# Convolution and Strassen-style block: POOL and SP work around the second group put in another order

## The chip, the cores and the metric

The kernel runs on one core of one Trainium2 chip. The metric is the device time of one execution in microseconds (us). Five engines work side by side, and each runs its own instructions in order: PE (matrix products, with PEld for its weight loads), DVE (vector work), ACT (activations and copies out of PSUM), POOL (general vector work, and the issue of some transfers) and SP (only the issue of transfers). A "granted clock" below 1.00 in a row of the profile means that PE was given a lower clock in that stretch.

## The reference, cut to what matters

```
# x: (8, 4224, 192), weight: (8 heads, 7 taps)
w = softmax(weight, axis=-1)                  # seven taps for each head of 24 columns
x = sum over k of w[h, k] * x_padded[s + k]   # causal convolution along the sequence
mu, var = mean(x), mean((x - mu) ** 2)        # over the 192 columns
xn = (x - mu) / sqrt(var + 1e-6) * g_ln
out = x + maximum(xn @ w_ch1, 0) @ w_ch2      # 192 -> 768 -> 192, float32
```

## The kernel before, in words

The sequence is cut into 18 groups. A group holds up to 16 rows of the sequence on each of 128 partitions. Group 0 has 6 rows and group 1 has 8, and these two are computed with plain products; groups 2 to 17 use a scheme that saves one of eight quarter products in each matrix multiplication and pays for it with sums and differences of quarters. The order of the work on every engine is written out by hand; no scheduler moves it. The semaphores are derived from which tile an instruction reads and writes.

For one group the steps are these.

- **Load**: `load_x(g)` brings x into a tile `xg`. There are two such tiles, so x of group 4 takes the place of x of group 2. The load of the fourth x (group 3) is special (`apart=True`): three transfers on SP (lines 165 and 172), the largest with 112 partitions.
- **Convolution**: `first_tap` (line 375, ACT) writes tap 0 into `y`; `second_tap` (line 383, ACT) writes tap 1 into a tile `tb`, and `third_tap`, for group 2 alone, writes tap 2 into a part of `room`. `add_in_parts` (line 408) adds one such tile to another by four accumulating transfers that POOL issues, 384 KB each. `conv` (line 416, DVE) adds the taps that are left, one instruction for each head and tap. `y` also has two tiles; groups 0 and 1 share the first, so `first_tap(3)` must wait until `y` of groups 0 and 1 has been stored.
- **Statistics**: `moments` (DVE) and `root` (POOL), a generator: it does nine small operations, stops once (`if step == 0: yield`), and does the other ten when it is asked again.
- **Store**: `store_y` writes `y` to the output, and later `add_to_out` (line 959, POOL) adds the scaled result to it with accumulating transfers. For group 1 `store_y` is eight transfers of 96 KB, since that group lies on 16 partitions per batch.
- **First product** (`up`, `up_mixed`, `up_last`, PE line 522) and its evictions by ACT (line 512 for groups 0 and 1, line 636 after). PSUM has two sets of four banks, taken in turn, so a product can't begin before ACT has emptied the set of the product before the last one. `between(g, f)` puts pieces of `first_tap(3)` behind the evictions of `up(1)`.
- **Second product** (`down`, PE line 812, for groups 0 and 1; `down_fast`, PE line 865, after).

The quarters of the weights have sums, too: `w1sums` (three) and `w2sums` (four), made once by `sums_of_quarters` on POOL (line 572). `let_in` is a DVE memset of one element on which such a sum then waits. In `up_mixed`, `close` adds one partial product to another: mostly ACT copies the PSUM banks out and POOL issues an accumulating transfer (line 600), once DVE adds (line 642). ACT then applies the relu (line 649), DVE forms a difference (`lower_sum`, line 841), and the second product starts on these.

The change touches four places. (1) The stretch under `if g == 0` and `if g == 1` in the main loop, where the work between `up(0)` and `up_mixed(2)` is ordered. (2) `up_mixed(2)`, where POOL issues `store_y(2)` and then makes `w2sums`, ahead of the transfers of `parts_cs` and `parts_tb`. (3) `between`. (4) `up_last`, where the result of group 16 is scaled and added to the output.

Of the kernel before, what the change touches and what calls it, by code (L numbers as in the profile page):

```python
# [16 lines left out]
def kernel(  # L17
# [29 lines left out]
    nc = tc.nc  # L47
# [318 lines left out]
    def first_tap(g, heads=(0, H)):  # L366
        n = groups[g][2]
        if g == 1:

            y[g] = y[0][:, groups[0][2] :]  # L370
        elif heads[0] == 0:
            y[g] = ypool.tile([P, J, D], F32, tag="y", name=f"y{g}")
        for h in range(*heads):
            cs = slice(h * GRP, h * GRP + GRP)
            nc.scalar.mul(y[g][:, 0:n, cs], xg[g][:, 0:n, cs], taps[:, h, 0:1])  # L375
# [21 lines left out]
    def third_tap(g, heads):  # L397
        if heads[0] == 0:
            third[g] = room[:, NF * J * Q + J * D :].rearrange("p (j d) -> p j d", d=D)
        tap_products(g, third[g], 2, heads)  # L400
        if heads[1] == H:
            add_in_parts(g, tb[g], third[g])

    def add_in_parts(g, dst, src):
        n = groups[g][2]
        for js in (slice(j, min(j + 4, n)) for j in range(0, n, 4)):
            ends = [v[:, js].rearrange("p j d -> p (j d)") for v in (dst, src)]
            nc.gpsimd.dma_start(out=ends[0], in_=ends[1], accum_op=ALU.add)  # L408
# [126 lines left out]

    def between(g, f):

        if g == 1 and f >= 3:
            first_tap(3, heads=[(0, 2), (2, 4), (4, H)][f - 3])
        if g == 1 and f == 5:  # L540
            second_tap(3)

# [28 lines left out]
    def sums_of_quarters(dst, a, b):  # L571
        nc.gpsimd.tensor_tensor(dst, a, b, op=ALU.subtract)  # L572
# [29 lines left out]
    def up_mixed(g, ahead, pending):  # L602
# [73 lines left out]
        p.close(p.c21, Y, two.c22[:, 0:1])  # L676
        if g == 2:
            store_y(g, nc.gpsimd)
            sums_of_quarters(w2sums[:, 2], b12, b22)
            sums_of_quarters(w2sums[:, 0], b12, b11)  # L680
            sums_of_quarters(w2sums[:, 1], b22, w2sums[:, 0])
            sums_of_quarters(w2sums[:, 3], b21, w2sums[:, 1])
        p.product(X, s4, p.b22, False)
        p.evict(X, p.c12, True)

# [48 lines left out]
    def up_last(g, ahead, pending):  # L734


        n = groups[g][2]
        w = n * T
        hidden_tile(g)
        a = ht[g]  # L740
        a11, a12, a21, a22 = quarters_of_y(g)
        s1, s2, s3, s4 = ysums[g]
        b11, b12, b21, b22 = quarters_of_w1()
        t = [w1sums[:, k] for k in range(3)]
        (c11, c12), (c21, c22) = [
            [a[:, h, e].rearrange("p f q j t -> p f q (j t)") for e in range(2)] for h in range(2)
        ]

        def seen(banks):
            return banks[:, :, 0 : FC * w].rearrange("p q (f w) -> p f q w", w=w)  # L750

        def product(to, left, right, first=True, end=True):
            rows_of_tiles(to, left, right, first, end, True)

        def close(c, banks):
            nc.vector.tensor_tensor(c, c, seen(banks), op=ALU.add)

        Y, X = take_set(), take_set()
        product(X, a11, b11, True, False)
        nc.scalar.copy(c11, seen(X))  # L760
        for step in range(2):
            next(pending, None)
        next(ahead)
        product(Y, a12, b21)
        close(c11, Y)
        size, step = groups[g - 1][2], 4

        def scaled(j):
            scale(g - 1, j, j + 1)
            if (j + 1) % step == 0:  # L770
                add_to_out(g - 1, j + 1 - step, j + 1)

        for j1 in range(0, HJ, step):
            part, factor = ots[g - 1][:, j1 : j1 + step], rstd[g - 1][:, j1 : j1 + step]
            nc.vector.tensor_tensor(
                part, part, factor.unsqueeze(2).to_broadcast([P, step, D]), op=ALU.mult
            )
            add_to_out(g - 1, j1, j1 + step)
        product(X, s2, t[0], False, False)
        nc.scalar.copy(c21, seen(X))  # L780
        product(Y, s3, t[1], True, False)
        nc.scalar.copy(c22, seen(Y))
        nc.scalar.activation(c11, c11, AF.Relu)
        product(X, s1, b12, False, False)
        close(c22, X)
        product(Y, a22, t[2], False)
        close(c21, Y)
        product(X, s4, b22, False)
        scaled(HJ), scaled(HJ + 1)
        nc.scalar.activation(c22, c22, AF.Relu)  # L790
        scaled(HJ + 2), scaled(HJ + 3)
        nc.scalar.activation(c12, seen(X), AF.Relu)
        lower_sum(g, (PAIR, *range(PAIR)))
        kept = xpool.tile([P, J + PAD, D], F32, tag="xg", name=f"kept{g}")
        kept = kept.rearrange("p j d -> p (j d)")[:, 0 : NF * (n - fast[g]) * P]
        kept = kept.rearrange("p (j e f q h t) -> p j e f q h t", e=2, f=FC, q=NQ, h=2, t=T)
        rows_left[g] = kept.rearrange("p j e f q h t -> p j (e f) (q h t)")

        def keep(h, e, j):
            nc.scalar.activation(  # L800
                kept[:, j - fast[g], e, :, :, h], a[:, h, e, :, :, j], AF.Relu
            )

        return [lambda j=j: scaled(j) for j in range(HJ + step, size)] + [
            lambda h=h, e=e, j=j: keep(h, e, j)
            for h, e in ((0, 0), (0, 1), (1, 1), (1, 0)) for j in range(fast[g], n)
        ]
# [142 lines left out]
    def add_to_out(g, j1, j2):  # L950
        if groups[g][0] is None:

            j1, j2 = (0, j2) if j2 == groups[g][2] else (0, 0)
        for ps, rows in rows_of_out(g, j1, j2) if j2 else ():
            src = ots[g][ps, j1:j2].rearrange("p j d -> p (j d)")
            step = 4 * D if groups[g][0] is not None else (j2 - j1) * D
            for d0 in range(0, (j2 - j1) * D, step):
                d1 = min(d0 + step, (j2 - j1) * D)
                nc.gpsimd.dma_start(out=rows[:, d0:d1], in_=src[:, d0:d1], accum_op=ALU.add)  # L959
# [65 lines left out]
    b11, b12, b21, b22 = quarters_of_w2()  # L1025
    for g in range(NG):
        last = g + 1 == NG
        if g + 2 < NG and g not in (1, 2):
            load_x(g + 2)
        if g < 2:  # L1030
            up(g)
            work = []
        else:
            work = (up_last if last else up_mixed)(g, ahead(g), pending)
            pending = iter(())
        if g == 0:
            early = CH * C // GRP
            join_low(*words_2)
            conv(1, 1, 5, heads=(0, early))
            join_sign(*words_2)  # L1040
            join_product(w2flat, *words_2)
            conv(1, 5, K, heads=(0, early))
            transpose(1, 0, CH)
            conv(1, heads=(early, H))
            first_tap(2)
            second_tap(2)
            let_in(w1sums[:, 1])
            sums_of_quarters(w1sums[:, 1], w12, w22)
            sums_of_quarters(w1sums[:, 0], w11, w1sums[:, 1])
            load_x(3, apart=True, gate=True)  # L1050
            transpose(1, CH, NC)
            store_y(1)
            moments(0)
            moments(1)
            down(g)
            for step in root(0):
                pass
            continue
        if g == 1:
            conv(2, 3)  # L1060
            flat = [v.rearrange("p j d -> p (j d)") for v in (y[2], tb[2])]
            nc.vector.tensor_tensor(flat[0], *flat, op=ALU.add)
            let_in(w1sums[:, 2])
            sums_of_quarters(w1sums[:, 2], w21, w1sums[:, 0])
            load_x(4, nc.gpsimd)
            transpose(2)
            fourth_sum = sums_of_y(2, nc.gpsimd)
            nc.vector.tensor_tensor(w12, w12, w11, op=ALU.subtract)
            moments(2)
            down(g)  # L1070
            fourth_sum()
            continue
        if g + 2 < NG:
            store_y(g + 1)
        results = down_fast(g, work)
        if last:
            finish_fast(g, 1, *results)
            for j in range(fast[g]):
                add(g, j, ots[g][:, j])
            store(g, 0, fast[g])  # L1080
            for j in range(fast[g], groups[g][2]):
                rows = take_bank()[:, 0:D]
                down_row(rows, lambda f: rows_left[g][:, j - fast[g], f])
                add(g, j, rows)
                store(g, j, j + 1)
        elif g % 2 == 0:
            pending = root(g)
# [30 lines left out]
```

## Time and profile before

| what | value |
|---|---|
| three runs | 960.52, 963.00, 963.14 us; median 963.0 |
| the profiled execution | 961.25 us, of which the span is 959.5 us |
| PE busy | 943.5 us, 98% of the span |
| DVE busy | 895.2 us, 93% |
| ACT busy | 720.2 us, 75% |
| POOL busy | 352.8 us, 37% |
| mean granted clock | 0.998 |

The page gives the busy time of each engine over the whole span. The list of waits names, for each line, what ended the idle time in front of its instructions. The timeline lists instructions in order of time, with equal neighbours merged: start, duration, engine, line, operation, output and input, count, and in brackets the idle time before the first of them and what ended it. A DMA row on an engine is the issue of a transfer, not the transfer; a row's landing time says when its data had arrived. A row of a stretch of time gives the busy time of each engine in it, the granted clock, the share of time in which the 16 DMA engines were busy, and the bytes moved per time. Spans on POOL are rough: a row begins when the instruction is taken up, also while the one before it is still at work.

### The profile page before, as it was taken

How to read it: one execution, taken by the hardware profiler on the slowest of the kernel's cores; microseconds unless marked ns; L12 is line 12 of the kernel's file. 1: busy time of each engine (PE TensorE's matmuls, PEld its weight loads, DVE VectorE, ACT ScalarE, POOL GpSimd, SP SyncE). 2: the span in 40 equal slices, each digit the busy share in tenths (PEclk: the TensorE clock that was granted, in tenths of full speed). 3: DMA queues.
4: the chain of work that ended last, by engine and by line, in shares of the span. 5: the costliest groups of instructions: out<-in, count | busy, mean ns of one | idle time of the engine just before them, and what ended most of it. 6: DMA issues, size and time to landing. Idle time of an engine off the chain costs nothing.

```text
span 959.5 us, 38510 instructions
## 1 busy us (share of the span) xinstructions
PE 943.5 (98%) x17106; PEld 745.2 (78%) x17106; DVE 895.2 (93%) x1479; ACT 720.2 (75%) x1283; POOL 352.8 (37%) x464
## 2 busy tenths in 40 slices
PE   9989899999999999999999999999999999999998
PEld 7989659687786978778695877769696877869687
DVE  8999789999999999999998999999999999997886
ACT  6955687969687896968778696877879697878654
POOL 2076556142544217141452416241361424332140
PEclk9999999999999999999999999999999999999999
DMA  8388787897969798897969889797978979685623
GB/s 203 120 190 198 181 243 141 232 179 163 238 134 265 137 244 156 198 221 130 276 125 258 154 197 206 134 268 144 251 150 227 186 149 228 134 175 112 111 36 78
DMA packets 38348, 171.94 MB, mean 179 GB/s; under 512 B 4517, under 2 KB 5798, under 8 KB 32039
## 3 DMA queue, kind: packets, MB, share of 16 engines
q0 software_dynamic: 31632, 109.03, 61.1%
q1 hardware_dynamic: 6544, 60.45, 17.3%
q8 instruction: 134, 2.20, 0.9%
q14 instruction: 32, 0.26, 0.1%
q10 hardware_dynamic: 6, 0.00, 0.0%
HBM read 38.92 MB, written 50.92 MB: 94 GB/s over the span
## 4 chain that ended last, share of the span: by engine, by line
PE 88%; DVE 4%; POOL 2%; DMA 2%; issue 2%; ACT 1%; DVEq 0%; POOLq 0%; ACTq 0%
PE ps L865 44%; PE ps L522 41%; DVE y L416 3%; PE ps L812 2%; POOL w2sums L572 1%; DMA room<-parts_tb 1%; PE ps L362 1%; DMA room<-parts_cs 1%; PE ps L323 1%; DVE st L447 0%; DMA room<-room 0%; POOL room L600 0%; ACT room L649 0%; PE ps L349 0%; ACT room L636 0%
## 5 line engine op out<-in xcount | busy, mean ns | idle before, releaser
L416 DVE SCALAR_TENSOR_TENSOR y<-xg,taps,y 128x384 f32<-128x384 f32 (+3 forms) x710 | 358.3, 579 | 0.6 <-issue 0.6
L865 PE MATMUL ps<-room,w2sums 128*32 128x256 f32 (+1 forms) x4464 | 244.0, 376 | 1.1 <-ACT cs L871 1.1
L636 ACT COPY room<-ps 128x512 f32<-128x512 f32 (+1 forms) x225 | 180.6, 845 | 63.4 <-PE ps L522 62.5
L522 PE MATMUL ps<-yt,w 32*128 32x256 f32 (+3 forms) x4092 | 226.1, 365 | 1.4 <-issue 0.9
L865 PEld LDWEIGHTS ps<-room,w2sums 128*32 128x32 f32 x4464 | 146.1, 110 | 93.1 <-ACT cs L871 2.0
L522 PEld LDWEIGHTS ps<-yt,w 32*128 32x128 f32 x4092 | 203.2, 185 | 19.0 <-issue 8.0
L865 PE MATMUL ps<-room,w 128*32 128x256 f32 (+1 forms) x3456 | 193.0, 375 | 4.4 <-ACT room L649 4.4
L908 DVE TENSOR_TENSOR room<-room 128x1024 f32<-128x1024 f32 x135 | 154.6, 1218 | 19.7 <-PE ps L865 14.2
L865 PEld LDWEIGHTS ps<-room,w 128*32 128x32 f32 x3456 | 112.1, 111 | 76.9 <-ACT room L649 5.3
L959 POOL DMA_DIRECT2D out_dram<-ot x70 | 59.9, 942 | 198.8 <-ACT ot L948 186.9
L522 PE MATMUL ps<-ysums,w1sums 32*128 32x256 f32 (+1 forms) x2304 | 132.2, 371 | 0.0
L522 PEld LDWEIGHTS ps<-ysums,w1sums 32*128 32x128 f32 x2304 | 121.2, 185 | 5.3 <-issue 0.2
L948 ACT ACTIVATE ot<-ot,r 128x192 f32<-128x192 f32 x246 | 104.2, 467 | 0.0
L649 ACT ACTIVATE room<-room 128x1024 f32<-128x1024 f32 x90 | 94.9, 1064 | 12.1 <-DMA room<-parts_cs 10.1
L871 ACT COPY cs<-ps 128x256 f32<-128x256 f32 (+1 forms) x192 | 70.8, 369 | 44.1 <-PE ps L865 43.6
L408 POOL DMA_DIRECT2D y<-tb x59 | 52.3, 1381 | 112.8 <-ACT room L871 97.3
L375 ACT ACTIVATE y<-xg,taps 128x384 f32<-128x384 f32 (+3 forms) x141 | 72.7, 606 | 4.8 <-DVE y L416 4.3
L522 PE MATMUL ps<-yt,w1sums 32*128 32x256 f32 (+1 forms) x1152 | 71.7, 371 | 0.0
L522 PE MATMUL ps<-ysums,w 32*128 32x256 f32 (+1 forms) x1152 | 71.2, 369 | 0.0
L447 DVE BATCH_NORM_STATS2 st<-y 128x6 f32<-128x192 f32 x264 | 70.2, 344 | 0.0
L871 ACT COPY room<-ps 128x256 f32<-128x256 f32 (+1 forms) x96 | 35.4, 371 | 40.4 <-PE ps L865 39.8
L383 ACT ACTIVATE tb<-xg,taps 128x384 f32<-128x384 f32 (+1 forms) x120 | 65.5, 625 | 0.0
(125 smaller groups left out, 977.0 us busy)
## 6 DMA issues: line engine op xcount, KB each, us to landing
xg<-in_x_dram SPq DMA_DIRECT2D x13, 2112.0 KB, 16.3
out_dram<-ot POOLq DMA_DIRECT2D x61, 384.0 KB, 9.5
room<-room POOLq DMA_DIRECT2D x45, 512.0 KB, 5.3
y<-tb POOLq DMA_DIRECT2D x58, 384.0 KB, 8.5
out_dram<-y SPq DMA_DIRECT2D x14, 1536.0 KB, 8.7
room<-parts_cs POOLq DMA_DIRECT2D x30, 512.0 KB, 6.8
room<-parts_tb POOLq DMA_DIRECT2D x15, 1024.0 KB, 7.6
xg<-in_x_dram POOLq DMA_DIRECT2D x1, 2112.0 KB, 13.0
```

The costliest lines, as they stand in the source:

```text
L375: nc.scalar.mul(y[g][:, 0:n, cs], xg[g][:, 0:n, cs], taps[:, h, 0:1])
L383: nc.scalar.mul(dst[:, 0:n, cs], xg[g][:, k : k + n, cs], taps[:, h, k : k + 1])
L416: nc.vector.scalar_tensor_tensor(out=y[g][:, 0:n, cs], in0=t[:, k : k + n, cs], scalar=taps[:, h, k : k + 1], in1=y[g][:, 0:n, cs], op0=AL ...
L447: nc.vector.bn_stats(out=sums[g][:, j, :], in_=y[g][:, j, :])
L522: nc.tensor.matmul(banks[:, q, i * w + j1 * t : i * w + j2 * t], right[rows, c, P * i : P * i + P], left[rows, j1:j2, c, :], start=start, ...
L636: nc.scalar.activation(to, of, AF.Relu) if relu else nc.scalar.copy(to, of)
L649: nc.scalar.activation(c, c, AF.Relu)
L865: nc.tensor.matmul(dst[C * q : C * q + C, 0:w], right[:, f, C * c : C * c + C], left[:, f, q], start=(first and f == PAIR), stop=(f == PAI ...
L871: nc.scalar.copy(to[:, c], dst[:, 0:w].rearrange("p (j t) -> p j t", t=t))
L908: nc.vector.tensor_tensor(dst[:, f], left[:, f], right_of[:, f], op=op)
L948: nc.scalar.mul(ots[g][:, j, :], ots[g][:, j, :], rstd[g][:, j : j + 1])
L959: nc.gpsimd.dma_start(out=rows[:, d0:d1], in_=src[:, d0:d1], accum_op=ALU.add)
```

## The change

- `third_tap(2)` no longer issues the four transfers that add the third tap to the second; POOL now does so between the two parts of `root(0)`.
- `store_y(1)` (eight transfers) stands ahead of `load_x(3)` (three) in SP's order.
- `first_tap(3)` is cut 1, 2, 2 and 3 heads behind the evictions 2, 3, 4 and 5 of `up(1)`, where it was 2, 2 and 4 behind 3, 4 and 5.
- The third sum of w1 moves on POOL from behind the y transfers of group 3 to directly behind `root(0)`, and its `let_in` memset goes.
- x of group 4 is loaded by SP at the head of pass `g == 2`, not by POOL in pass `g == 1`.
- The four sums of w2 move on POOL from `up_mixed(2)`, behind `store_y(2)`, to the end of pass `g == 1`, ahead of all transfers of `up_mixed(2)`.
- In `up_last`, DVE scales and adds one piece of four rows of group 16, not two; the rows 4 to 7 are scaled by ACT between its copies, one place earlier than the rows behind them, which move back.

```diff
         tap_products(g, third[g], 2, heads)
-        if heads[1] == H:
-            add_in_parts(g, tb[g], third[g])
...
-        if g == 1 and f >= 3:
-            first_tap(3, heads=[(0, 2), (2, 4), (4, H)][f - 3])
+        if g == 1 and f >= 2:
+            first_tap(3, heads=[(0, 1), (1, 3), (3, 5), (5, H)][f - 2])
...
             store_y(g, nc.gpsimd)
-            sums_of_quarters(w2sums[:, 2], b12, b22)
-            sums_of_quarters(w2sums[:, 0], b12, b11)
-            sums_of_quarters(w2sums[:, 1], b22, w2sums[:, 0])
-            sums_of_quarters(w2sums[:, 3], b21, w2sums[:, 1])
...
-        for j1 in range(0, HJ, step):
-            part, factor = ots[g - 1][:, j1 : j1 + step], rstd[g - 1][:, j1 : j1 + step]
-            nc.vector.tensor_tensor(
-                part, part, factor.unsqueeze(2).to_broadcast([P, step, D]), op=ALU.mult
-            )
-            add_to_out(g - 1, j1, j1 + step)
+        part, factor = ots[g - 1][:, 0:step], rstd[g - 1][:, 0:step]
+        nc.vector.tensor_tensor(
+            part, part, factor.unsqueeze(2).to_broadcast([P, step, D]), op=ALU.mult
+        )
+        add_to_out(g - 1, 0, step)
         product(X, s2, t[0], False, False)
         nc.scalar.copy(c21, seen(X))
+        scaled(step), scaled(step + 1)
...
         product(X, s4, b22, False)
-        scaled(HJ), scaled(HJ + 1)
+        scaled(step + 2), scaled(step + 3)
         nc.scalar.activation(c22, c22, AF.Relu)
-        scaled(HJ + 2), scaled(HJ + 3)
+        for j in range(HJ, HJ + step):
+            scaled(j)
...
-        if g + 2 < NG and g not in (1, 2):
+        if g + 2 < NG and g != 1:
             load_x(g + 2)
...
             sums_of_quarters(w1sums[:, 0], w11, w1sums[:, 1])
+            store_y(1)
             load_x(3, apart=True, gate=True)
             transpose(1, CH, NC)
-            store_y(1)
             moments(0)
             moments(1)
             down(g)
-            for step in root(0):
-                pass
+            steps = root(0)
+            next(steps)
+            add_in_parts(2, tb[2], third[2])
+            next(steps)
+            sums_of_quarters(w1sums[:, 2], w21, w1sums[:, 0])
             continue
...
-            let_in(w1sums[:, 2])
-            sums_of_quarters(w1sums[:, 2], w21, w1sums[:, 0])
-            load_x(4, nc.gpsimd)
             transpose(2)
...
             fourth_sum()
+            sums_of_quarters(w2sums[:, 2], b12, b22)
+            sums_of_quarters(w2sums[:, 0], b12, b11)
+            sums_of_quarters(w2sums[:, 1], b22, w2sums[:, 0])
+            sums_of_quarters(w2sums[:, 3], b21, w2sums[:, 1])
             continue
```

## The prediction

> **What bounds the kernel now.** First the page's busy times, then the waits of PE.
>
> ```profile
> PE 943.5 (98%) x17106; PEld 745.2 (78%) x17106; DVE 895.2 (93%) x1479; ACT 720.2 (75%) x1283; POOL 352.8 (37%) x464
> PE ps L865 <- ACT room L649: 4.4, 2, 2.7
> PE ps L812 <- ACT room L512: 2.4, 1, 2.4
> ```
>
> PE is busy for all but 16 us of the span. Besides start, end and single gaps of about 1 us there are two waits: 2.4 us before the second product of group 1 and 4.4 us before that of group 2. The change touches both places. Next, PE's timeline and the clock around the larger one, and what POOL and DVE did before it.
>
> ```profile
> 111.17 0.64 PE L865 MATMUL ps<-room,w 128*32 128x256 f32 x8
> 114.55 0.64 PE L865 MATMUL ps<-room,w 128*32 128x256 f32 x8 [2.75 <-ACT room L649]
> 116.83 4.92 PE L865 MATMUL ps<-room,w 128*32 128x256 f32 x56 [1.64 <-ACT room L649]
> ...
> 117.00:120.40 3.40, 3.40 (x36) 1.74 (x32) 3.40 (x6) 3.40 (x5) 0.00 (x0) 0.50 0.56 113
> ...
> 93.56 0.87 POOL L488 DMA_DIRECT2D out_dram<-y  x1
> 94.13 10.26 POOL L572 TENSOR_TENSOR w2sums<-w 128x288 f32<-128x288 f32 x2
> 104.47 2.73 POOL L572 TENSOR_TENSOR w2sums<-w,w2sums 128x288 f32<-128x288 f32 x2
> 107.14 1.77 POOL L600 DMA_DIRECT2D room<-parts_cs  x2
> ...
> 88.09 14.88 DVE L416 SCALAR_TENSOR_TENSOR y<-xg,taps,y 128x384 f32<-128x384 f32 x28
> ...
> 98.33 1.93 ACT L636 COPY parts_cs<-ps 128x1024 f32<-128x1024 f32 x2 [0.72 <-PE ps L522]
> 104.00:108.00 4.00, 4.00 (x80) 3.79 (x76) 4.00 (x4) 3.37 (x2) 3.84 (x5) 1.00 0.00 0
> ```
>
> ACT had parts_cs out of PSUM at 100.26; POOL issued its transfers only at 107.14, since the w2 sums held it from 94.43 to 107.19. From 104 to 108 the DMA engines did nothing (share 0.00). The transfers landed at 113.36 and 115.70, the relus followed, and PE waited. The two gaps then brought a granted clock of 0.50 for 3.4 us, the only such stretch: this product's 488 matmuls took 28.23 us by the chain of waits, while 504 take 27.33 later (26.46 for 488). So this place costs 4.4 + 1.8 = 6.2 us.
>
> The smaller wait:
>
> ```profile
> 60.01 1.02 ACT L512 ACTIVATE room<-ps 128x1024 f32<-128x1024 f32 x1 [1.56 <-PE ps L522]
> 65.38 1.12 ACT L375 ACTIVATE y<-xg,taps 128x384 f32<-128x384 f32 x2 [4.34 <-DVE y L416]
> 66.41 1.00 ACT L512 ACTIVATE room<-ps 128x1024 f32<-128x1024 f32 x1
> 67.31 1.11 ACT L375 ACTIVATE y<-xg,taps 128x384 f32<-128x384 f32 x2
> 68.32 1.01 ACT L512 ACTIVATE room<-ps 128x1024 f32<-128x1024 f32 x1
> ...
> 47.30 0.81 SPq L165 DMA_DIRECT2D xg<-in_x_dram  x2
> 48.44 11.80 SPq L488 DMA_DIRECT2D out_dram<-y  x8
> ```
>
> Two evictions of up(1) stand on ACT behind first_tap(3), which started at 65.38. The row names DVE, but what it waits for there, the moments, ended at 51.9. The late ones are the stores of y: the last three were issued at 57.55 to 59.45, as each reuses a semaphore of the x transfers ahead of it, and landed by about 64.9. PE's sixth matmul of down(1) needs the last eviction (69.33); unhindered, behind five of 0.33 from the end of up(1) at 65.06, it would have run at 66.7. The place costs 2.6 us.
>
> **The change part by part.**
>
> *w2 sums (PE's second wait).* They now follow the last y sum on POOL. Removed: the hold of 94.43 to 107.19. Added at the new place: four operations of 0.66 us (the first ended at 103.64, 0.66 after DVE fell idle at 102.97) to 0.99. Where that is follows from DVE's chain, so the third sum of w1 comes first.
>
> *Third tap's transfers and the third w1 sum.* POOL runs nine root operations from 53.7 at one per 0.53 us (their spacing now, beside L416): to 58.5. Then four transfers at 0.84 (3.34/4): to 62. Ten more root operations: to 67.3. Then the w1 sum, 2.65 us. Beside DVE's running L416 it either gets in at once and holds DVE, or waits for conv(2,3) to end at 69.6; both end about 72.2. The transfers' packets needed 8.2 us of all DMA engines before (57.5 on, last landing 69.42); from about 60 that gives a landing near 71, also before 72.2. So the flat add (3.36 us, now at 69.79) starts at about 72.2: 2.4 late. In exchange L592 shrinks from 5.06 us (it lay beside this same w1 sum) to L591's 0.96, 4.1 less. So moments(2) ends 86.4, not 88.17: DVE 1.7 us early. yt is ready at 78.9 (PE wants it at 83), s2 at 80.9 (wanted at 85): cost 0.
>
> *The w2 sums there.* POOL's two y sums (1.83 each) end at about 85.9; the first w2 sum runs beside the moments, the other three meet conv(3) from 86.5. Before, the last two did the same: L416 became 1.14 instead of 0.605, 0.54 each. So POOL is free at about 89.8 and DVE loses 1.6, its lead. L600's first issue slips from 87.90 to 89.8; its relu is wanted only at 102.7 and the landing takes 8, so this is hidden. parts_cs then goes out at 98.9 and 99.9, when ACT is done. It queues behind store_y(2), whose packets end at 103.8 as now, and by the 6.2 us from issue to landing of an empty queue lands near 108 and 110. Relus at 109 and 111.3; PE wants the second at 111.17 + 0.9. Stall 0 to 1, taken as 0.2. With no gap, no half clock: **-6.0 us**, bounds -6.2 and, if the stall stays at one 2.75 us gap without the clock, -3.4.
>
> *Stores ahead of x, finer first_tap.* SP issues eight stores from 47.30 at 0.46: x leaves at 51.1 instead of 47.30. Its three transfers landed 11.8 to 12.1 after the first issue; same DMAs, so 62.9 to 63.2, and ACT starts first_tap(3) at about 63.5. Then one head (0.52), eviction 3 (0.9), two heads (1.0), eviction 4 (0.9), two heads (1.0), eviction 5 (1.0): the sixth matmul runs at start + 5.4 = 68.9 against 69.38. **-0.5 us.** But eviction 3 now stands behind the wait: PE product 5 starts at start + 1.6 = 65.1 instead of 62.4, a PE gap of 2.7. If that trips the half clock, 1.7 is lost. Bounds: -2.6 (x by 61) to +1.7 (clock) or, x landing 2 later, +1.5.
>
> *x of group 4 on SP*: issued when conv(2) ends, 69.6, while the DMA share is 0.02 (69 to 76). Landed 93.56 before, ahead of the first L600; it is used at 128.9. Worth nothing by itself; SP's next work is at 122.8, so nothing is queued behind it. The y transfers (ACT's second tap ends 74.4, 75.4 before) stand beside its tail; landing 86 to 87.5, before 86.74. conv(3) has 1.6 us of cover. 0, bounds 0 to +1.5.
>
> *up_last*: DVE loses one L775 (0.95). ACT's two 0.46 scales fit in its 0.90 idle ahead of the copy at 927.62; rows 8 to 11 fit into the 1.80 idle ahead of 936.62. The additions (0.9 on POOL) end at 942.3 as before; the span ends with L963 and a store. 0, bounds -0.9 to +0.5 (the 0.92 PE gap at 933.76 has no named cause).
>
> Sum: 961.25 - 6.0 - 0.5 = 954.8, with the half clock in up(1) 956.5. The profiled execution lies 1.75 under the median 963.0 of the runs, a spread of the size of one half-clock stretch. I take 955.8.
>
> [...] In the trace the first w2 sum waited 8.5 us through sixteen L416, while the last two got in at the next L416. [...] In the trace PE gaps of 2.75 and 1.64, split by 0.64 of work, brought the half clock. [...]
>
> **Rivals.**
> 1. *POOL is shut out by DVE (slower).* If the second w2 sum waits like the first did, until conv(3) pauses at 101.4, POOL gives L600 its first issue at about 104; the third lands near 114 instead of 100.93, ACT's eviction of c22 (103.64) waits for that, and PE stands some 10 us where it stood 4.4: 961.25 + 5 = 966. For it: the 9.50 us span. Against: back-to-back sums got in at the next instruction, and two of three start at the head of conv(3). It decides if the wait exceeds some 8 us. Chance 0.16.
> 2. *A new wait takes half of the gain*: y of group 3 lands after 89, or x after 65, or parts_cs stays behind the store; PE still stands 2 to 3 us. 961.25 - 3 = 958.5 to 961. For it: DMA share 1.03 from 85 to 98. Chance 0.18.
> 3. *The stall stays as it is*, since the sums were not what parts_cs waited for (the store in front of them ran to 103.8): 961 to 963. Against: DMA share 0.00 from 104 to 108. Chance 0.08.
>
> **How the numbers follow.** The likeliest case (0.58) has 952.5 to 958 as its own range. Rivals 2 and 3 reach to 963; with rival 1 left out the range is 952.0 to 963.0. A difference under 0.3% (2.9 us: 960.1 to 965.9) can't be told from none. Faster: 0.58 + 0.14 of rival 2 = 0.72; same: 0.04 of it and 0.08 = 0.12; slower: 0.16.
>
> **What the profile after would show.** Right: no idle row in front of the second product of group 2, no 0.50 stretch there, w2sums before the first L600, its transfers of parts_cs at 98 to 100; first_tap(3) at 63 to 64; L592 at 0.96. Wrong: a w2sums row of many us, L600 after 95, idle PE rows released by room or ps around 62 to 69 above 3 us, or conv(3) starting after 89.

## The result, and the profile after

The changed kernel takes 957.81 us (median of six runs, 955.85 to 960.04); the kernel before, run beside it, 963.07 (960.26 to 965.12). The ratio is 0.9952, with a 95% interval of 0.9929 to 0.9975: about 5 us faster. The profiled execution took 957.02 us with a span of 955.3, against 961.25 and 959.5.

The busy times of the page after:

```profile
PE 942.7 (99%) x17106; PEld 749.6 (78%) x17106; DVE 891.6 (93%) x1477; ACT 720.4 (75%) x1287; POOL 343.7 (36%) x463
```

PE is busy for 0.8 us less than before, and idle for 12.6 instead of 16. The larger new rows in the list of PE's waits after (us in total, times, longest us):

```profile
PE ps L520 <- ACT room L510: 3.5, 2, 3.2
...
PE ps L860 <- issue: 1.4, 3, 0.7
```

The two waits that stood there before, 4.4 us at the second product of group 2 and 2.4 at that of group 1, are gone. In their place there is one of 3.2 inside `up(1)`, where PE had none, and three short ones in the last second product that no engine ended. PE's timeline after shows the first of them and the mended place:

```profile
50.02 13.23 PE L520 MATMUL ps<-yt,w 32*128 32x256 f32 x240
66.41 4.50 PE L520 MATMUL ps<-yt,w 32*128 32x256 f32 x48 [3.16 <-ACT room L510]
70.84 15.87 PE L807 MATMUL ps<-w,room 128*128 128x192 f32 x96
...
111.37 2.96 PE L520 MATMUL ps<-yt,w 32*128 32x256 f32 x48
114.26 4.09 PE L860 MATMUL ps<-room,w 128*32 128x256 f32 x72
118.17 7.95 PE L860 MATMUL ps<-room,w2sums 128*32 128x256 f32 x144
```

The row of a stretch in the same profile (busy time of PE, PEld, DVE, ACT and POOL, then granted clock, DMA share, GB/s):

```profile
66.40:69.80 3.40, 3.39 (x32) 2.87 (x36) 3.40 (x5) 2.88 (x5) 3.23 (x4) 0.50 0.96 183
```

The sixth product of `up(1)` waits 3.16 us for ACT, and its 48 matmuls then take 4.50 us at a clock of 0.50, where 48 of the 288 took 2.64 before (15.82/6). In front of the second product of group 2 (114.26), and in it, there is neither an idle row nor a slow stretch. The timelines of ACT and POOL after tell why, in both places:

```profile
58.20 1.02 ACT L510 ACTIVATE room<-ps 128x1024 f32<-128x1024 f32 x1 [1.56 <-PE ps L520]
64.83 0.61 ACT L375 ACTIVATE y<-xg,taps 128x384 f32<-128x384 f32 x1 [5.61 <-POOL d L476]
65.35 1.00 ACT L510 ACTIVATE room<-ps 128x1024 f32<-128x1024 f32 x1
...
86.05 1.55 POOL L570 TENSOR_TENSOR w2sums<-w 128x288 f32<-128x288 f32 x2
87.67 1.67 POOL L570 TENSOR_TENSOR w2sums<-w,w2sums 128x288 f32<-128x288 f32 x2
90.99 0.87 POOL L598 DMA_DIRECT2D room<-room  x1 [1.65 <-ACT room L634]
...
102.73 1.76 POOL L598 DMA_DIRECT2D room<-parts_cs  x2 [5.21 <-ACT parts_cs L634]
```

The fourth eviction of `up(1)` (65.35; number 3 in the diff and the prediction, which count from 0) stands behind a first_tap(3) that started only at 64.83. The row names POOL, but the wait that ended last on ACT there, at 64.56, is on a transfer of x, as the chain of work that ended last has it:

```profile
51.73 12.80 DMA xg<-in_x_dram
64.53 0.03 ACTq L375
```

The w2 sums are done at 89.34, ahead of every addition, and `parts_cs` goes out as soon as ACT has it; it lands at 109.71 and 112.25. DVE's timeline after, for steps 2 and 3 of the prediction:

```profile
72.41 3.36 DVE L1060 TENSOR_TENSOR y<-y,room 128x3072 f32<-128x3072 f32 x1 [0.19 <-issue]
...
80.27 0.96 DVE L590 TENSOR_TENSOR ysums<-ysums,yt 128x768 f32<-128x768 f32 x1
...
82.43 4.25 DVE L445 BATCH_NORM_STATS2 st<-y 128x6 f32<-128x192 f32 x16
89.01 15.04 DVE L414 SCALAR_TENSOR_TENSOR y<-xg,taps,y 128x384 f32<-128x384 f32 x28 [2.33 <-ACT room L634]
```

PE's time cut at the places that the change touches, from the starts of the products in the timelines:

| stretch of PE | before | after | difference |
|---|---|---|---|
| start to `up(1)` | 49.24 | 50.02 | +0.8 |
| `up(1)` and `down(1)` | 34.3 | 36.6 | +2.3 |
| `up_mixed(2)` | 27.6 | 27.6 | 0 |
| second product of group 2 | 33.8 | 27.3 | -6.5 |
| groups 3 to 16 | 772.2 | 770.9 | -1.3 |
| `up_last` to PE's last matmul | 37.6 | 38.2 | +0.6 |

Together, unrounded, that is -4.2, the whole difference of the spans. The change takes out 6.5 us and gives 2.3 back, 48 us earlier. The experiments ask what each part is worth by itself, and why the sum of the parts is not the whole.

### The profile page after: what moved, and what is told of

The parts are those of the page before. It is cut to its first block, busy times and chain, and to the rows that moved or that the text cites. A ratio compares the mean times of both kernels' runs of the same rounds, so it can differ in the third digit from the quotient of the medians.

```text
span 955.3 us, 38512 instructions
## 1 busy us (share of the span) xinstructions
PE 942.7 (99%) x17106; PEld 749.6 (78%) x17106; DVE 891.6 (93%) x1477; ACT 720.4 (75%) x1287; POOL 343.7 (36%) x463
## 4 chain that ended last, share of the span: by engine, by line
PE 90%; DMA 3%; DVE 2%; POOL 2%; ACT 1%; issue 1%; SPq 0%; ACTq 0%; DVEq 0%; POOLq 0%
PE ps L860 44%; PE ps L520 41%; PE ps L807 2%; DVE y L414 2%; DMA xg<-in_x_dram 1%; DMA room<-room 1%; PE ps L362 1%; ACT room L634 1%; PE ps L323 1%; POOL room L598 0%; POOL d L457 0%; SPq L486 0%; POOL r L480 0%; POOL d L475 0%; POOL d L476 0%
## 5 line engine op out<-in xcount | busy, mean ns | idle before, releaser
L634 ACT COPY room<-ps 128x512 f32<-128x512 f32 (+1 forms) x225 | 180.6, 844 | 63.9 <-PE ps L520 62.4
L860 PEld LDWEIGHTS ps<-room,w2sums 128*32 128x32 f32 x4464 | 148.7, 110 | 90.1 <-issue 1.6
L860 PE MATMUL ps<-room,w 128*32 128x256 f32 (+1 forms) x3456 | 190.5, 373 | 0.2 <-DVE room L640 0.2
L866 ACT COPY room<-ps 128x256 f32<-128x256 f32 (+1 forms) x96 | 35.7, 372 | 40.4 <-PE ps L860 39.7
```

Source lines behind the costliest of these rows:

```text
L634: nc.scalar.activation(to, of, AF.Relu) if relu else nc.scalar.copy(to, of)
L860: nc.tensor.matmul(dst[C * q : C * q + C, 0:w], right[:, f, C * c : C * c + C], left[:, f, q], start=(first and f == PAIR), stop=(f == PAI ...
L866: nc.scalar.copy(to[:, c], dst[:, 0:w].rearrange("p (j t) -> p j t", t=t))
```

## The experiments

Each comparison had runs of the kernel before beside it; their medians were 963.59 us in the first (first four kernels), 961.50 in the second (next four) and 961.98 in the third. Ratios are to these.

### The new wait in up(1): three ways to order the same work

**x ahead of the stores again, first_tap(3) cut as before.**

```diff
-            store_y(1)
             load_x(3, apart=True, gate=True)
             transpose(1, CH, NC)
+            store_y(1)
...
-        if g == 1 and f >= 2:
-            first_tap(3, heads=[(0, 1), (1, 3), (3, 5), (5, H)][f - 2])
+        if g == 1 and f >= 3:
+            first_tap(3, heads=[(0, 2), (2, 4), (4, H)][f - 3])
```

> The changed kernel with the x transfers ahead of the stores again and first_tap(3) cut 2, 2, 4 behind evictions 3, 4, 5, all else as changed. Theory (the new order of this step is what costs: the fourth eviction of up(1) stands behind a first_tap that waits for x, PE stands 3.16 us and then runs 48 matmuls at half clock in 4.50 instead of 2.64): up(1) runs without a gap, first_tap(3) starts at about 65.5, the wait moves to the sixth matmul of down(1) with about 2, and down(1) ends near 83.6 instead of 86.7: 957.8 - 3.1 = 954.7. Rival (the transfers of the third tap, now beside x, are what makes the eviction late, whatever the order on SP): PE still loses what it lost, 957 or more.

Measured: 958.4 us, ratio 0.9947 (0.9929 to 0.9965), no better than the changed kernel. The gap did move, but it brought the slow clock with it. Timelines of PE and ACT, then the row of the stretch:

```profile
66.63 17.56 PE L807 MATMUL ps<-w,room 128*128 128x192 f32 x96 [2.58 <-ACT room L510]
...
64.55 1.12 ACT L375 ACTIVATE y<-xg,taps 128x384 f32<-128x384 f32 x2 [4.78 <-DMA out_dram<-y]
```

```profile
68.00:71.40 3.40, 3.40 (x13) 3.24 (x12) 3.15 (x4) 3.40 (x7) 1.18 (x1) 0.50 0.15 30
```

`up(1)` and `down(1)` take 36.1 us, and first_tap(3) now waits for the last stores. Undoing both halves of the step brings nothing, against my theory. The time fits the rival (957 or more), but the row names the last stores, not x, as what ACT waited for. The packets of the third tap's transfers ran beside these stores from 58.8 on; whether they made the stores late isn't shown. That they make the eviction late whatever the order on SP, as the rival has it, falls with the next kernel.

**The cut of first_tap(3) alone undone, the stores still ahead of x.** The diff is the second half of the one above.

> The changed kernel with first_tap(3) cut 2, 2, 4 behind evictions 3, 4, 5 again; the stores stay ahead of x. Theory (the place of first_tap ahead of the fourth eviction costs, not the order on SP): no gap in up(1), no half clock there, first_tap(3) still at about 64.8, the sixth matmul of down(1) at 68.8 with a gap of about 1.3, down(1) ends near 83.0 instead of 86.7: 957.8 - 3.7 = 954.1. Rival (the order on SP costs, since x lands 1.5 later than forecast): 956.5 or more.

Measured: 953.46 us, ratio 0.9899 (0.9875 to 0.9922), 4.4 under the changed kernel. Timelines of ACT and PE:

```profile
62.59 1.12 ACT L375 ACTIVATE y<-xg,taps 128x384 f32<-128x384 f32 x2 [2.38 <-POOL r L480]
...
64.67 16.16 PE L807 MATMUL ps<-w,room 128*128 128x192 f32 x96 [0.24 <-ACT room L510]
```

So the new order on SP is a gain, 4.9 us between these two kernels: first_tap(3) starts 14.2 us after the start of `up(1)` (48.42) instead of 16.6 (47.98) in the kernel above. The loss is the one head of first_tap that was put ahead of the fourth eviction: PE gets 0.24 us of waiting without it, 3.16 with it.

**The whole of first_tap(3) behind the last eviction.**

```diff
-        if g == 1 and f >= 2:
-            first_tap(3, heads=[(0, 1), (1, 3), (3, 5), (5, H)][f - 2])
+        if g == 1 and f == 5:
+            first_tap(3)
```

> The changed kernel with the whole of first_tap(3) behind eviction 5 of up(1). Theory: no eviction waits for x or for a store, PE has no gap from 50.0 to the end of down(1) at 81.8 (5.0 earlier): 957.8 - 5.0 = 952.8; ACT's first and second tap take 66.9 to 75.1, the y transfers leave at about 75.2 instead of 77.9. Rival (a new wait takes what is won: conv(3), the sums of w2 and the transfers of parts_cs were in time only because PE came late): PE stands again before the second product of group 2 or waits for y sums, 955.5 to 958.

Measured: 953.02 us, ratio 0.9893 (0.9869 to 0.9916). `up(1)` and `down(1)` take 32.1 us and the second product of group 2 27.3, so no new wait appeared. first_tap(3) starts at 65.58, and ACT is through with it and second_tap(3) at 73.8 instead of 77.6. The rival's wait is there in small in other profiles: four kernels of the last groups below share this order, and in theirs PE waits 0.3 to 1.7 us in front of that product for DVE (line 640). This and the kernel above it cannot be told apart.

### What the place of the w2 sums is worth

**The w2 sums back in up_mixed(2), all else as changed.** The four calls stand behind `store_y(2)` again.

> The changed kernel with the four sums of w2 back behind store_y(2) in up_mixed(2). Theory (these sums were what held the transfers of parts_cs): they span about 12.8 us behind the store at 97, parts_cs leaves at about 110, PE stands some 4.4 at the second product of group 2 and runs a stretch at half clock: 957.8 + 6.2 = 964.0. Rival (the store in front of the sums, or the later third tap, decides when parts_cs lands): within 1 of 957.8.

Measured: 960.01 us, ratio 0.9965 (0.9950 to 0.9980), 2.2 over the changed kernel (1.3 by the ratios) instead of 6.2. The profile shows no stall at all (timelines of POOL and PE):

```profile
97.37 7.72 POOL L570 TENSOR_TENSOR w2sums<-w 128x288 f32<-128x288 f32 x2
...
106.80 1.73 POOL L598 DMA_DIRECT2D room<-parts_cs  x2
...
114.40 4.13 PE L864 MATMUL ps<-room,w 128*32 128x256 f32 x72
```

The sums held `parts_cs` until 106.80, as before (107.14). But PE, having lost time in `up(1)`, came to the second product at 114.40 instead of 111.17, and what landed at 111.36 and 114.13 was in time. In the changed kernel the two parts cover the same stall: the loss of the one makes most of the gain of the other. The median of ten runs is still 2.2 above; that may be a stall in runs other than the profiled one, which the profile doesn't show.

**The same with PE in time (the whole of first_tap(3) last).**

> The kernel with the whole of first_tap(3) behind eviction 5, and the four sums of w2 back behind store_y(2) in up_mixed(2). Theory (with the sums there the stall was hidden only while PE came 5 us late from up(1)): parts_cs leaves near 106 and lands near 110 and 113, PE wants it at 108.6 and 109.2, stands some 4 to 5 and runs a stretch at half clock: 953.0 + 6 = 959.0. Rival (the sums' place is worth no more than the 2.2 by which the same edit moved the changed kernel): 955.2.

Measured: 958.1 us, ratio 0.9964 (0.9947 to 0.9981), 5.1 over the same kernel with the sums moved (6.8 by the ratios). The size is what the theory gave, the mechanism is another (timelines of POOL, DVE and PE):

```profile
91.38 1.87 POOL L570 TENSOR_TENSOR w2sums<-w 128x288 f32<-128x288 f32 x2
...
96.88 1.77 POOL L598 DMA_DIRECT2D room<-parts_cs  x2 [1.48 <-ACT parts_cs L634]
...
88.72 17.68 DVE L414 SCALAR_TENSOR_TENSOR y<-xg,taps,y 128x384 f32<-128x384 f32 x28 [2.34 <-ACT room L634]
...
111.37 4.09 PE L864 MATMUL ps<-room,w 128*32 128x256 f32 x72 [2.90 <-DVE room L640]
```

Here the sums got in at once between conv's instructions and were done at 95.4, so `parts_cs` was not held. They held DVE: the 28 instructions of conv(3) took 17.68 us instead of 14.91 in the kernel with the sums moved, DVE's addition L640 came that much later, and PE waited 2.90 for it, without a slow clock.

**The kernel before with the w2 sums moved, and nothing else.**

> The kernel before with one part of the change alone: the four sums of w2 stand behind the last y sum of pass g == 1. Here they meet conv(3), which starts at 88.1 as before. Theory (each sum waits for one of conv's instructions, as the last two did before): POOL is free near 91.5, the first addition goes out about 3.5 later than at 87.90 but in time, parts_cs goes out at 98 to 99, PE has no wait and no half clock at the second product of group 2: 963.6 - 6.2 = 957.4, with the 2.4 before the second product of group 1 left. Rival (POOL is shut out by DVE): a w2sums row of 8 us or more at 88 to 104, the first addition after 100, PE stands longer than before, 966 or more.

Measured: 957.6 us, ratio 0.9962 (0.9942 to 0.9981), so 3.9 under its neighbour and not 6.2. The sums meet conv(3) here, and POOL is not shut out (timelines of POOL, DVE and PE):

```profile
87.87 1.86 POOL L572 TENSOR_TENSOR w2sums<-w 128x288 f32<-128x288 f32 x2
89.81 2.06 POOL L572 TENSOR_TENSOR w2sums<-w,w2sums 128x288 f32<-128x288 f32 x2
91.82 2.64 POOL L600 DMA_DIRECT2D room<-room  x3
...
88.42 16.57 DVE L416 SCALAR_TENSOR_TENSOR y<-xg,taps,y 128x384 f32<-128x384 f32 x28
...
113.12 3.28 PE L861 MATMUL ps<-room,w 128*32 128x256 f32 x56 [0.58 <-ACT room L649]
```

conv(3) takes 16.57 instead of 14.88; three of its instructions are 1.15 long instead of 0.61. PE's second product of group 2 takes 28.3 us (27.3 free of waits), 5.5 less than before, at full clock. By the profile the part is worth 5.5, by the medians 3.9.

**The kernel before with the stores ahead of x and the finer first_tap(3), and nothing else.**

> The kernel before with one part of the change alone: the stores of group 1 ahead of x and first_tap(3) cut 1, 2, 2, 3 behind evictions 2 to 5. Theory (the two waits are not additive, as PE's delay at up(1) gives POOL's sums of w2 the time they lack): up(1) and down(1) take some 2.3 longer, PE comes about 3 later to the second product of group 2, whose stall of 4.4 and half clock of 1.8 are gone or nearly: 963.6 + 2.3 - 6 = 959.9. Rival (the two places are independent and the stall stays): 963.6 + 2.3 = 965.9.

Measured: 963.96 us, ratio 1.0013 (0.9986 to 1.0040): no gain. Against its neighbour's 961.50 that is +2.5 (by the ratio +1.3, with an interval from -1.3 to +3.8), the rival's size (+2.3) and not the theory's (-3.7). Yet the stall did not stay; the timelines of PE and POOL and the row of the slow stretch show both halves:

```profile
66.48 5.41 PE L522 MATMUL ps<-yt,w 32*128 32x256 f32 x48 [3.63 <-ACT room L512]
...
98.21 8.45 POOL L572 TENSOR_TENSOR w2sums<-w 128x288 f32<-128x288 f32 x2
...
117.27 3.06 PE L865 MATMUL ps<-room,w 128*32 128x256 f32 x52 [0.96 <-ACT room L649]
```

```profile
64.90:71.70 6.80, 5.21 (x48) 3.99 (x48) 5.49 (x10) 4.46 (x7) 1.84 (x5) 0.50 0.68 131
```

`up(1)` and `down(1)` take 38.3 us, 4.0 more than before; the second product of group 2 takes 28.7, 5.2 less, although the w2 sums stand where they stood and `parts_cs` leaves even later, at 108.35. So the theory's mechanism is there, and its sum failed by a dearer `up(1)` (3.63 of gap and a slow stretch of twice the length), and in the profile also by 1.4 in the last groups (39.0 from `up_last` to PE's last matmul, 37.6 before): here a delay of PE of 4 us at `up(1)` removes most of the stall at group 2 by itself.

### The third tap and the third w1 sum

**The best kernel so far (first_tap(3) last) with this part undone.** The four transfers stand in `third_tap` again, the sum with its `let_in` behind the y transfers of group 3.

```diff
-            next(steps)
-            add_in_parts(2, tb[2], third[2])
-            next(steps)
-            sums_of_quarters(w1sums[:, 2], w21, w1sums[:, 0])
...
+            let_in(w1sums[:, 2])
+            sums_of_quarters(w1sums[:, 2], w21, w1sums[:, 0])
```

> The kernel with the whole of first_tap(3) behind eviction 5, and the third tap's four transfers and the third sum of w1 where they were before (transfers right behind the third tap, the sum behind the y transfers of group 3, with its let_in). Theory (this part costs and gains nothing, as forecast): 953, within 1; DVE's second difference lasts about 5 instead of 0.96, the moments of group 2 end within 2 of where they did, PE does not see it. Rival (moving it is worth something now that PE comes 5 earlier): y sums late for up_mixed(2), PE waits 2 to 4 for them or conv(3) runs later than the first relu allows, 955 to 957.

Measured: 956.6 us, ratio 0.9950 (0.9930 to 0.9970), 3.6 over the kernel it came from (5.5 by the ratios). The rival held. Timelines of POOL, DVE and PE:

```profile
77.34 3.93 POOL L572 TENSOR_TENSOR w1sums<-w,w1sums 128x1152 f32<-128x1152 f32 x1
...
91.85 2.63 POOL L600 DMA_DIRECT2D room<-room  x3
...
88.45 16.57 DVE L416 SCALAR_TENSOR_TENSOR y<-xg,taps,y 128x384 f32<-128x384 f32 x28
...
86.09 1.58 PE L522 MATMUL ps<-ysums,w1sums 32*128 32x256 f32 x24 [0.36 <-POOL ysums L596]
...
113.37 3.27 PE L862 MATMUL ps<-room,w 128*32 128x256 f32 x56 [1.83 <-ACT room L649]
```

With the w1 sum in its old place POOL's y sums end at 87.9 instead of 84.1, the w2 sums meet conv(3) again, the additions start at 91.85 instead of 87.25, and PE, which is in time here, waits in `up_mixed(2)` (28.8 us instead of 27.6) and for the relu of `parts_cs`.

### The last groups

**up_last as before, with first_tap(3) last**, twice, in two comparisons.

> The kernel with the whole of first_tap(3) behind eviction 5, and up_last as before (DVE scales and adds two pieces). Theory (the last product's waits for nothing that the profile names, 1.4 to 3.3 us against 0.9 before, come with the changed up_last): the part from up_last to the end of PE takes 37.6 again instead of 40.4: 953.0 - 2.5 = 950.5. Rival (they are the load of PE's program, whose phase the rest of the kernel sets): 953.0, within 0.7.

> The kernel with the whole of first_tap(3) behind eviction 5 and up_last as before, once more, beside the one with late additions: 951.2 as it was, with 37.5 for the part from up_last to the end of PE. If the theory of the program loads holds, it is some 1.5 slower than the one with late additions; if the order on DVE and ACT decides, 2 faster.

Measured: 951.19 us, ratio 0.9891 (0.9859 to 0.9923), and 952.91, ratio 0.9914 (0.9898 to 0.9930). The nine runs have a median of 952.9.

**One place for the late additions.** In `scaled`, the second, third and fourth addition are written behind the last scaled row.

```diff
-            if (j + 1) % step == 0:
-                add_to_out(g - 1, j + 1 - step, j + 1)
+            if j + 1 == size:
+                for j1 in range(step, size, step):
+                    add_to_out(g - 1, j1, j1 + step)
```

> The kernel with the whole of first_tap(3) behind eviction 5 and the changed up_last, but its second, third and fourth addition all wait until the last row of group 16 is scaled, so that three transfers stand together behind it. Theory of the program loads: only the last loads can be late, 37 instead of 40.4 for the part from up_last to the end of PE, 949.7. Rival (it is the changed order on DVE and ACT, not the transfers): 40.4 stays, 953.

Measured: 952.32 us, ratio 0.9904 (0.9886 to 0.9922). The edit did not do what it was for. Each addition waits only for its own rows, and POOL has nothing else to do there, so the three went out at 924.09, 927.83 and 933.12, as spread out as ever. It is a second run of the kernel with first_tap(3) last; the nine runs of the two have a median of 952.5. By the times the old and the new `up_last` can't be told apart.

**Without the four additions of group 16's result** (their transfers are left out, so that group's rows lack the product).

```diff
         def scaled(j):
             scale(g - 1, j, j + 1)
-            if (j + 1) % step == 0:
-                add_to_out(g - 1, j + 1 - step, j + 1)
...
-        add_to_out(g - 1, 0, step)
```

> The kernel with the whole of first_tap(3) behind eviction 5 and the changed up_last; it leaves out the four additions of group 16's scaled rows to the output in up_last (their transfers alone, not the scaling). Theory (PE's waits in the last two products are for loads of its own program, 128 matmuls each, and these loads come late because the additions' transfers, now spread over three places, are in their way): no load is late, PE has no gap there, and the part from up_last to the end of PE takes 36.3 instead of 40.4: 953.0 - 4 = 949. Rival (the transfers have nothing to do with it): 40.4 stays, 953.

Measured: 950.2 us, ratio 0.9881 (0.9863 to 0.9900); `up_last` to PE's last matmul takes 36.5 us instead of 40.4. PE's timeline in the second product of group 17, first with the additions (the kernel with the old cut of first_tap(3), which has the same `up_last`), then without:

```profile
927.24 4.44 PE L860 MATMUL ps<-room,w2sums 128*32 128x128 f32 x139
933.10 0.31 PE L860 MATMUL ps<-room,w2sums 128*32 128x128 f32 x3 [1.42 <-issue]
...
935.21 1.58 PE L860 MATMUL ps<-sums,w2sums 128*32 128x128 f32 x49
938.21 2.71 PE L860 MATMUL ps<-sums,w2sums 128*32 128x128 f32 x91 [1.42 <-issue]
```

```profile
927.39 4.11 PE L857 MATMUL ps<-room,w2sums 128*32 128x128 f32 x144
931.32 2.15 PE L857 MATMUL ps<-room,w 128*32 128x128 f32 x72
```

What these gaps are can be read from the trace. The page after, like the page before, has the row `q8 instruction: 134, 2.20, 0.9%`: 134 packets with 2.20 MB, so 16 KB each. PE has 17,106 matmuls and as many weight loads; if the packets are loads of their program, there is one for 128 matmuls with their weight loads (17,106/134 = 127.7). That they are is inferred from the name of the queue, from this count and from the borders: in every profile PE's unexplained gaps in the last two products lie where 573, 445, 317, 189 or 62 matmuls are left (one off in one profile), so 127 or 128 apart. The packets show, against these borders, where each load starts:

| kernel | loads start with so many matmuls left | gaps at (us) |
|---|---|---|
| before | 824, 600, 541, 419, 282, 148 | 573 (0.92) |
| after | 824, 663, 495, 389, 277, 145 | 445 (0.74), 317 (0.32), 189 (0.32) |
| old cut of first_tap(3) | 828, 665, 512, 345, 209, 141 | 317 (1.42), 189 (1.42) |
| without the additions | 828, 700, 568, 436, 268, 141 | none over 0.13 |

Without the additions the first loads start within 1 to 9 matmuls of the border (701, 573, 445) and two later ones 48 and 49 behind it (268 for 317, 141 for 189), none with a gap over 0.13. With them the loads come up to 120 late (325 for 445, in the kernel with late additions; 209 for 317 in the table). That the gaps are waits for these loads shows in their ends: at each of the 27 gaps over 0.2 us in the last 50 us of the fourteen profiles, PE goes on 1.2 to 1.6 us after the end of a packet. Shown is that with the additions these loads start late. How the additions delay one is not: the packets themselves took 0.9 to 1.9 us there in all kernels. By gaps over 0.2 us the old `up_last` pays at one border in three of five profiles and at two or three in the others, the new one at two or three in seven of eight; the stretch takes 37.3 to 39.0 (five, old) against 37.9 to 40.4 (eight, new), which the medians don't repeat.

## Why the prediction was right and wrong, step by step

The forecast was 955.8, from a sum of 954.8 for the profiled execution. The runs gave 957.8 and 957.0. Direction and range hold, and so does the own range of the likeliest case (952.5 to 958), at its edge; but one step had the wrong sign and another was right for a reason that is only half of the truth. Two of its own signs of being wrong were there: an idle PE row of 3.16 released by room in front of 66.41, and conv(3) starting after 89 (89.01). That the number came within about 2 us is in part luck: step 4 was 2.8 too low, and the w2 sums (0.5) and groups 3 to 16 (1.3, in no term) gave more than forecast.

1. **w2 sums, -6.0.** Measured -6.5 at that place, with everything that was named: no idle row, no 0.50 stretch, sums ahead of the first addition, `parts_cs` out when ACT is done (102.73, and not 98 to 100, since PE and ACT were 3 us later), landings in time. But the term was added as if it were independent of step 4. With the sums back the place loses 0.15 us by the profile as long as PE is late (27.48 against 27.33); alone in the kernel before the move is worth 5.5 by the profile and 3.9 by the medians. A delay of PE at `up(1)` and the relief of POOL pay for the same stall. The sum of the whole change isn't hurt by this, since with the sums moved there is no stall left for the delay to hide and it counts in full in step 4; but neither term is what its part is worth alone. By the ratios moving the sums is worth 1.3 us with PE late (0.9952 against 0.9965) and 6.8 with PE in time (0.9893 against 0.9964). The two parts alone moved the medians by -3.9 and +2.5, which makes -1.4, and the whole change by -5.3; other parts of the change and intervals of about 2 us each lie between, so these three medians by themselves wouldn't show it.
2. **Third tap and w1 sum, 0.** Every row came as worked out: the flat add at 72.41 (forecast 72.2), the second y sum 0.96, the moments' end at 86.68 (86.4). The w1 sum got in at once, the first of the two cases. Right for this kernel by these rows, though the step wasn't undone alone here: where PE is in time it is worth 3.6 (5.5 by the ratios).
3. **w2 sums beside conv(3), 1.6 of DVE.** It didn't arise: the sums ran in a pause of DVE from 86.68 to 89.01, which was luck, as conv(3) was forecast to start at 86.5. The bound was tested by the kernel that has them beside conv(3), and there it is close: 16.57 against 14.88, 1.7, and POOL free at 91.8.
4. **Stores ahead of x, -0.5.** Measured +2.3; this is the step that failed, a gain that came out as a loss. "But eviction 3 now stands behind the wait: PE product 5 starts at start + 1.6 = 65.1 instead of 62.4, a PE gap of 2.7. If that trips the half clock, 1.7 is lost" was the right mechanism, and I carried it as a bound instead of as the value. The gap was 3.16, and the half clock cost 1.86 (4.50 - 2.64). Of the two halves of the step the new order on SP gained (958.4 against 953.5, both with the old cut of first_tap(3)), and the finer cut lost (957.8 against 953.5, both with the new order). One size was off: first_tap(3) began at 64.83 and not at 63.5, as x took 13.2 us from its first issue to the end of ACT's wait (51.35 to 64.56), not 11.8 to 12.1; that `up(1)` began 0.8 later took a part of this back. The last packets of x (62.8 to 63.7) ran among those of the third tap's transfers, but step 2 isn't what made x late: in the kernel with this step alone, where these transfers stand in their old place, x took 13.5 (51.10 to 64.63). What made it late is open. Where PE waits was also misread: before, the gap of 2.40 lies in front of the first matmul of down(1) (67.46), right behind eviction 4 (ended 67.41), so it is the room in PSUM that is late first, and the data of eviction 5 only after it.
5. **x of group 4 on SP, 0.** The y transfers took 10.8 us from issue to last landing (77.88 to 88.64), 11.0 before, so the tail of x cost them nothing. conv(3) started at 89.01 and not before 88.1, because second_tap ended later (77.6 against 75.4), and PE did not wait for it. Unforeseen: the three profiles with this x on POOL have a PE gap of 1.1 us, ended by ACT's copies into `cs`, at 506 to 512, the eleven with it on SP have none. It belongs to the -1.3 of the middle groups; it wasn't tried alone, and its way is open.
6. **up_last, 0.** +0.6 in the profile. The gap of 0.92 that had no named cause is gone as a row, and three others are there in its place: at each, PE goes on 1.4 to 1.5 us after the end of a packet of the instruction queue, and without the additions no gap there is over 0.13 us.

**Rivals.** The first (POOL shut out, 966) did not happen in the changed kernel and falls in the kernel made for it. There the sums get in one conv instruction apart, and three of conv(3)'s instructions are 1.15 long instead of 0.61. It isn't so in every profile: the first w2 sum took 9.5 us before, 7.0 in the changed kernel with the w2 sums back, and 7.7 in the kernel before with the stores ahead of x, each time until conv(3) had ended. What decides between the two remained open. The second rival (a new wait takes a part of the gain, 958.5 to 961) named x as a possible cause and is the nearest to what happened: at 2.3 us it took a third, not half, and 957.8 lies just below its range. The third (the store held `parts_cs`) falls: with the store in front and the sums gone, the transfers leave on time.

**The clock.** I had one row, half clock after gaps of 2.75 and 1.64, and kept its price out of the sum. The runs show half clock after gaps of 2.58 (x ahead of the stores again), 2.61 (the w2 sums back, 48 matmuls in 4.56 us) and 3.16 (the change), and two stretches (6.8 us) after 3.63 (the stores alone); none after 2.09 (the w2 sums alone), 2.40 (before) and 2.90 (the w2 sums back with PE in time). Length alone doesn't decide. The slow stretches of the rows above are 3.4 us long or twice that, and one starts 1.4 us after work has begun again (68.0 after 66.63); what sets the start is not shown. As an estimate from these rows, a gap of 2.6 us costs 1.7 us on top of itself (17.56 against 15.87 for the 96 matmuls of down(1)); no run shows one of 2.6 without this price.

## What to carry to other kernels

Don't add gains and losses on one chain as if they were independent: work out the arrival times at the next meeting point again with every step applied, since a delay upstream can hide a stall downstream, and while it does, mending the stall shows little (here 1.3 us instead of 6.8 by the ratios). Before work is put into an in-order queue ahead of the emptying of a buffer, ask what that work waits for; here one head of 0.5 us in front of an eviction cost 4.4 us, and putting all of first_tap(3) behind the last eviction gave the better kernel (953.0 against 957.8, and 963.6 before). Waits named "issue" lay at borders 127 or 128 matmuls apart here and ended 1.2 to 1.6 us after a packet of the instruction queue, and the transfers beside them belonged to their price (in the profiles 40.4 us from `up_last` to PE's last matmul with the additions, 36.5 without).

## What was not expected of the hardware

- The instruction queue brought 134 packets of 16 KB in the profiles before and after, by the count one for 128 of PE's 17,106 matmuls and their weight loads. While additions to the output ran, these loads came up to 120 matmuls late, and PE stood for up to 2.0 us at a border; without these transfers it stood for 0.13 at most.
- How long a small operation on POOL lasted beside a running row of DVE instructions differed between profiles. In the kernel with first_tap(3) last, one of `root(0)`'s operations behind the third tap's issues took 8.7 us (59.88 to 68.57), until conv(2) had ended (68.52); in the changed kernel the same one took 1.8.
- A gap of 2.90 us brought no slow stretch (the 72 matmuls behind it, in the kernel with first_tap(3) last and the w2 sums back, took 4.09 us, as they did in the changed kernel without a gap), and one of 2.58 halved the clock for 3.4 us (68.00 to 71.40).
